# Reordering the first loads of a two-stage convolution kernel, and moving 18 outputs from its direct part to its triples

## The chip, the cores and the metric

One Trainium2 chip, one core. The metric is the device time of one execution in microseconds (us). Every profile shown is of one execution; its span is counted from the first instruction of the program to the last, and the execution's own time is a little longer than the span.

## The reference

Two 5-tap convolutions over time, each followed by GELU and by dropping every second output, then a joint network: projections of the result and of a second input `g`, their sum for every pair of positions, tanh, and an output projection.

```python
h = sum(einsum("btc,cd->btd", xp[:, i:i+T, :], w1[i]) for i in range(5))   # xp: x padded by 2
h = gelu(h)[:, ::2, :]
f = sum(einsum("btc,cd->btd", hp[:, i:i+T1, :], w2[i]) for i in range(5))  # hp: h padded by 2
f = gelu(f)[:, ::2, :]
fe, ge = f @ w_f, g @ w_g
out = tanh(fe[:, :, None, :] + ge[:, None, :, :]) @ w_o
```

Here B = 2, T = 4000, D = 512, 8 positions of `g`; the output is 2 x 1000 x 8 x 512 in bf16. T1 = 2000 and T2 = 1000.

## The kernel before

**Who does what.** TensorE (PE) does the matrix products, VectorE (DVE) and ScalarE (ACT) the sums, copies and nonlinear functions, GpSimd (POOL) memsets and sums late in the kernel, and the SyncE queue (SP) issues all loads and nearly all stores.

**An order made by a planner.** The program lists operations with what they read and write. `Plan` gives each a modelled cost, derives the dependencies, runs a list scheduler many times while it shifts priorities, and writes the resulting fixed order of instructions for each engine, with the semaphore waits that the dependencies need. Engines run their lists in order: an instruction that waits holds up everything behind it on its engine. So an edit in one place can change the order of ACT and DVE well after it.

**The first convolution in three kinds of parts.** Outputs of batch 0 begin with `ND` = 468 outputs computed directly, tap by tap (`direct`). The rest goes in triples: three outputs at a time by nine products in place of fifteen (`Triple` and `Unit`; the nine are t2, tm, sm, t1, s1, t0, s0, ti, si). A unit is one 128-wide slice of output channels of one triple part, four units to a part. The first, small triple part has `NF` = 176 columns a product (buffer `xa`), the second, `NL` = 336 columns (`xp1`), covers the end of batch 0. Batch 1 is two parts of 334 columns (`xp2`, then `xp0`). `NL` follows from the other two, `2 * 334 - ND / 3 - NF`.

**The direct part.** It needs samples with even and odd positions apart and channels on the partitions (`eo`). The samples come in two loads of 512 (`xr0`, `xr1`, called first and second samples here); each is transposed on PE (`turn(rt, pp, ...)`, `rt` the load, `pp` even or odd, eight transposes a call) and copied from PSUM to `eo`, in two halves of the channels, by DVE and ACT. Even taps need the even samples, odd taps the odd ones. `direct(i, lo, hi)` issues 16 matmuls (four output slices by four input slices) for tap `i` and outputs `lo` to `hi`. Outputs up to `NH` = 254 need the first samples alone.

**The order of the taps and loads.** `TAPS = (0, 4, 2, 1, 3)`. SP issues `xr0`, the weights of tap 0, `xr1`, the weights of tap 4, of tap 2, then transposing loads of `xa` with the weights of taps 1 and 3 among them, then those of `xp1`, `xp2` and `xp0` (six planes each), a small one called `xe` that holds the last samples of batch 1, and the weights of the second convolution. A load made with an `after` argument is issued only when an earlier load has landed: that of tap 4 waits for `xr0`, that of tap 2 for tap 0.

**Weights for the triples.** While PE is in the direct part, DVE and ACT combine the taps of `w1` into the weights that the triples use: `w1part(m, "04")` needs taps 0 and 4, `w1part(m, "213")` the others. They also form the sums of samples (`row` and the planes themselves, `Triple.step`).

**A unit's path.** t2 goes into a PSUM bank and ACT copies it out (`sd<-acc`); tm and sm are added to the bank and ACT copies it out again; t1 and s1 are added; DVE then forms the other two results (`acc<-acc,sd`, `sd<-acc,sd`), and t0, s0 and ti, si follow. Each step on PE needs the copy or sum before it. ACT's final function writes `hT`.

**The rest.** The second convolution (again triples, over `hT`), the projections and the joint network follow. Nothing of them is edited.

Of the kernel before, what the change touches and what calls it, by code (L numbers as in the profile page):

```python
# [360 lines left out]
def bass_standalone__seq2seq_rnn_t_joint__speech_kernel(  # L361
# [23 lines left out]
    assert (B, T, D, K, U) == (2, 4000, 512, 5, 8)  # L385
    T1, T2 = T // 2, T // 4
    NT3 = (T2 + 2) // 3
    ND, NF = 468, 176
    NL = 2 * NT3 - ND // 3 - NF
    assert ND % 6 == 0 and NF % 2 == 0 and NL % 2 == 0  # L390
    EW = 16 + 4 * P
# [7 lines left out]
    TAPS = (0, 4, 2, 1, 3)  # L399
    NX = 2  # L400

    with ExitStack() as es:
# [72 lines left out]
        pl = Plan(nc)  # L475
        sub, add = ALU.subtract, ALU.add

        def vec_cost(o, ins, fast=True):
            bf = fast and all(not v.psum and v.ap.dtype in (BF16, FP16) for v in (o,) + tuple(ins))
            return o.ap.free_size() * (0.52e-3 if bf else 1.04e-3) + 0.065  # L480
# [8 lines left out]
        def act(o, i, func, scale=1.0, bias=None):  # L489
            rd = (i,) if bias is None else (i, bias)  # L490
            pl.op("act", lambda e: e.activation(o.ap, i.ap, func, scale=scale,  # L491
                                                bias=0.0 if bias is None else bias.ap), rd, (o,),
                  o.ap.free_size() * 0.833e-3 + (0.05 if i.psum else 0.105 if bias is None else 0.186))

        def mm(o, pairs, start, stop, check=True):

            def fn(e):
                for n, (l, r) in enumerate(pairs):
                    ins = e.matmul(o.ap, lhsT=l.ap, rhs=r.ap, start=start and n == 0,  # L499
                                   stop=stop and n == len(pairs) - 1, skip_group_check=not check)  # L500
                return ins
            pl.op("pe", fn, [v for pr in pairs for v in pr], (o,), len(pairs) * max(o.ap.free_size() / 2400 + 0.0028, 0.056))
# [13 lines left out]
        def load_w(eng, dst, src, slack=0.0):  # L516
            return pl.dma(eng, lambda e: e.dma_start(dst.ap, src), (), (dst,), slack=slack)

        def load_xr(rt):
            dst = xr[rt][:].map(lambda a: a.rearrange("p r k c -> p (r k c)"))  # L520
            src = x[0, 4 * P * rt:4 * P * (rt + 1), :].rearrange("(p r) c -> p (r c)", r=4)
            return pl.dma("sp", lambda e: e.dma_start(dst.ap, src), (), (dst,), rate=370e3)

        def load_x6(buf, b, ph, j0, col, n=336, slack=1.0):

# [3 lines left out]
            return pl.dma("sp", lambda e: e.dma_start_transpose(out=dst.ap, in_=src), (), (dst,), nbytes=n * 2 * D, rate=175e3, slack=slack)  # L529

        came = [load_xr(0)]
        act(warm[0:1], warm[1:2], ACT.Gelu_apprx_tanh)

        def load_w1(i, after=None):
            o = load_w("sp", w1_sb[i], w1[i].rearrange("(k c) d -> c k d", c=P))
            if after is not None:
                o.after.append(after.idx)
            return o
# [3 lines left out]
        def load_a(*phs):  # L542
            for ph in phs:
                load_x6(xa, 0, ph, JA, 0, 16 * -(-(NF + 2) // 16), 0.8)

        came.append(load_w1(TAPS[0]))
        came.append(load_xr(1))
        for i in TAPS[1:3]:
            came.append(load_w1(i, came[-3]))
        load_a(4, 0)  # L550
        came.append(load_w1(TAPS[3], came[-3]))
        load_a(2)
# [33 lines left out]
        def turn(rt, pp, cost):  # L586
            for h in range(2):
                bk = 4 * (rt ^ pp) + 2 * h + 1
                pv = View(psb[:, bk * 1024:bk * 1024 + 512].rearrange("p (r k c) -> p r k c", r=2, k=2), np.array([bk]), True)

                def fn(e, pv=pv, h=h):
                    for k in range(2):
                        for r in range(2):
                            ins = e.transpose(pv.ap[:, r, k, :], xr[rt].h[:, 2 * r + pp, 2 * h + k, :], ident.h[:, :])  # L594
                    return ins
                pl.op("pe", fn, (xr[rt][:], ident[:]), (pv,), cost)
                lo = 16 + 2 * P * rt
                o = eo[pp, 2 * h:2 * h + 2, lo:lo + 2 * P].map(lambda a: a.rearrange("p k (c r) -> p k c r", r=2))
                v = pv.map(lambda a: a.rearrange("p r k c -> p k c r"))
                if h or rt and pp:  # L600
                    act(o, v, ACT.Copy)
                else:
                    pl.op("dve", lambda e, o=o, v=v: e.tensor_copy(out=o.ap, in_=v.ap), (v,), (o,), vec_cost(o, (v,)))
# [157 lines left out]
        NH = 2 * P - 2  # L761

        def direct(i, lo=0, hi=ND):
            for m in range(NK):
                mm(ps.cols(2 * m * NT + lo, hi - lo),
                   [(w1_sb[i, k, m * P:(m + 1) * P], eo[i % 2, k, 15 + i // 2 + lo:15 + i // 2 + hi]) for k in range(NK)],
                   i == TAPS[0] and lo == 0, i == TAPS[-1], False)
# [7 lines left out]
        turn(0, 0, 0.43)  # L775
        direct(TAPS[0], 0, NH)
        turn(0, 1, 0.43)
        turn(1, 0, 0.22)
        direct(TAPS[0], NH, ND)
        turn(1, 1, 0.22)  # L780
        for i in TAPS[1:]:
            direct(i)
        for m in range(NK):
            v = ps.cols(2 * m * NT, ND).map(lambda a: a.rearrange("p (q r) -> p r q", r=6))
# [503 lines left out]
```

## Time and profile before

| | |
|---|---|
| runs | 253.19, 253.51, 252.77 us |
| median | 253.19 us |
| profiled execution | 253.5 us, its span 251.7 us |
| granted TensorE clock | 0.999 |
| PE busy | 246.3 us, 98% of the span |
| DVE, ACT busy | 211.8 and 211.7 us, 84% each |
| POOL busy | 97.5 us, 39% |
| moved by DMA | 31.99 MB, mean 127 GB/s; 234, 277 and 241 GB/s in the first three of 40 slices, 6.3 us each |

How to read the views: "PE" is TensorE's matmuls, "PEld" its weight loads, which run beside them. A row of the timeline gives start, length, engine, line, operation, output and inputs with partitions and elements, and in brackets how long the engine had been idle and what ended that. The chain of waits goes back from the last instruction, at each step to what released it. All helper matmuls have line 499, all ACT functions line 491. A row's length is from start to end; instructions of one engine overlap at their ends, so what a step costs its engine is the distance between starts.

### The profile page before, as it was taken

To read this page: it belongs to the slowest core of one execution; us is meant where nothing else is said; L and a number is where in the kernel's file an instruction comes from. 1 tells how busy PE (TensorE), PEld (TensorE's weight loads), DVE (VectorE), ACT (ScalarE), POOL (GpSimd) and SP (SyncE) were. 2 spreads that over 40 slices of the span, in tenths; PEclk is the share of its full clock that TensorE was granted. 3 is DMA by queue.
4 is the path that set the end of the run, shared out by engine and by line. 5 is a ranking of instruction groups with operands and counts; after the bars stand their busy time and mean duration, and the time that the engine had idled before them with its cause. 6 is when DMAs were issued, how large, how long until landed. Compare 5 with 4: busy or idle time off the path is not lost.

```text
span 251.7 us, 5281 instructions
## 1 busy us (share of the span) xinstructions
PE 246.3 (98%) x1909; PEld 180.3 (72%) x1915; DVE 211.8 (84%) x354; ACT 211.7 (84%) x356; POOL 97.5 (39%) x105
## 2 busy tenths in 40 slices
PE   8999999999999999999999999999999999999995
PEld 4646986666666666667556878777888878787883
DVE  2699998965999999398966878899999995889773
ACT  3496999659968766984499999999999999999872
POOL 1000000000000000000006987879999998878750
PEclk9999999999999999999999999999999999999999
DMA  6999999998300034000001033432335365555457
GB/s 234 277 241 189 175 146 154 182 171 297 125 0 3 0 112 142 0 1 3 0 0 39 5 128 108 133 99 83 126 118 177 128 212 193 180 183 177 147 172 226
DMA packets 55159, 31.99 MB, mean 127 GB/s; under 512 B 32062, under 2 KB 54878, under 8 KB 55134
## 3 DMA queue, kind: packets, MB, share of 16 engines
q1 hardware_dynamic: 54846, 31.47, 47.6%
q8 instruction: 15, 0.25, 0.4%
q10 hardware_dynamic: 288, 0.20, 0.3%
q14 instruction: 10, 0.08, 0.1%
HBM read 7.86 MB, written 16.38 MB: 96 GB/s over the span
## 4 chain that ended last, share of the span: by engine, by line
PE 73%; ACT 16%; issue 4%; DMA 4%; SPq 1%; DVE 1%; POOL 0%; ACTq 0%; DVEq 0%
PE acc L499 73%; ACT sn L1016 4%; DMA xr<-in_x_dram 3%; ACT jX L491 2%; ACT jT L491 2%; ACT row L491 2%; ACT sd L491 1%; ACT og L1016 1%; DMA xe<-in_x_dram 1%; SPq L529 1%; ACT ost L1016 1%; ACT hT L491 1%; DVE og L486 1%; ACT xp L491 0%; PE acc L594 0%
## 5 line engine op out<-in xcount | busy, mean ns | idle before, releaser
L486 DVE TENSOR_TENSOR og<-acc,sn 128x512 bf16<-128x512 f32 x84 | 55.0, 684 | 10.6 <-PE acc L499 8.9
L491 ACT ACTIVATE jT<-feT,geT 128x1000 bf16<-128x1000 f32 (+6 forms) x56 | 52.7, 1003 | 0.3 <-DVE feT L486 0.3
L499 PE MATMUL acc<-tw,ss 128*128 128x256 f16 x336 | 46.1, 273 | 0.1
L1079 POOL TENSOR_TENSOR ss<-jT 128x512 f16<-128x512 bf16 x25 | 29.0, 1169 | 38.9 <-DVE ss L1079 37.6
L499 PE MATMUL acc<-row,w_sb 128*128 128x334 bf16 (+2 forms) x224 | 38.8, 295 | 0.0
L499 PEld LDWEIGHTS acc<-tw,ss 128*128 128x128 f16 x336 | 32.4, 98 | 7.5 <-ACT sn L1016 0.5
L1016 ACT ACTIVATE sn<-acc 128x512 f32<-128x512 f32 x51 | 33.1, 655 | 2.6 <-PE acc L499 1.7
L499 PE MATMUL acc<-wo_sb,jT 128*128 128x256 bf16 (+1 forms) x187 | 31.3, 292 | 0.3
L499 PEld LDWEIGHTS acc<-row,w_sb 128*128 128x128 bf16 x224 | 21.1, 97 | 9.5 <-DVE acc L606 0.9
L491 ACT ACTIVATE jX<-feT,geT 128x1000 bf16<-128x1000 f32 (+4 forms) x28 | 25.2, 970 | 0.0
L1017 DVE COPY sn<-acc 128x512 f32<-128x512 f32 x33 | 22.2, 684 | 2.7 <-PE acc L499 2.4
L483 POOL MEMSET hT<- 128x8 bf16 (+2 forms) x6 | 0.8, 149 | 59.1 <-ACT hT L491 43.1
L499 PEld LDWEIGHTS acc<-wo_sb,jT 128*128 128x128 bf16 x192 | 18.7, 98 | 6.1
L491 ACT ACTIVATE hT<-acc 128x334 bf16<-128x334 f32 (+3 forms) x36 | 15.2, 438 | 9.0 <-PE acc L499 8.8
L491 ACT ACTIVATE sd<-acc 128x334 f32<-128x334 f32 (+2 forms) x48 | 19.7, 431 | 3.5 <-PE acc L499 2.8
L606 DVE SCALAR_TENSOR_TENSOR acc<-acc,sd 128x334 f32<-128x334 f32 (+2 forms) x24 | 11.6, 483 | 10.1 <-PE acc L499 10.0
L1079 POOL TENSOR_TENSOR ss<-jX 128x512 f16<-128x512 bf16 x16 | 18.5, 1159 | 3.5 <-DVE ss L1079 3.5
L486 DVE TENSOR_TENSOR row<-row 128x1336 bf16<-128x1336 bf16 (+2 forms) x24 | 19.0, 795 | 0.0
L499 PE MATMUL acc<-xp,w_t 128*128 128x334 bf16 (+1 forms) x96 | 17.6, 305 | 0.0
L499 PE MATMUL acc<-hT,w_t 128*128 128x334 bf16 x96 | 17.6, 304 | 0.0
L499 PE MATMUL acc<-wo_sb,ss 128*128 128x256 bf16 x112 | 17.0, 273 | 0.0
L499 PE MATMUL acc<-xp,w_x 128*128 128x334 bf16 (+1 forms) x96 | 16.9, 305 | 0.0
(124 smaller groups left out, 512.3 us busy)
## 6 DMA issues: line engine op xcount, KB each, us to landing
out_dram<-og SPq DMA_DIRECT2D x98, 128.0 KB, 2.0
w_sb<-in_w_dram SPq DMA_DIRECT2D x10, 512.0 KB, 5.7
out_dram<-ost SPq DMA_DIRECT2D x10, 128.0 KB, 1.9
xr<-in_x_dram SPq DMA_DIRECT2D x2, 512.0 KB, 4.8
wf_sb<-in_w_f_dram SPq DMA_DIRECT2D x1, 512.0 KB, 3.6
wg_sb<-in_w_g_dram SPq DMA_DIRECT2D x1, 512.0 KB, 4.7
wo_sb<-in_w_o_dram SPq DMA_DIRECT2D x1, 512.0 KB, 5.8
xp<-in_x_dram SPq DMA_TRANSPOSE x18, 4.8
```

Of the source, the lines that this page charges most:

```text
L483: pl.op("pool", lambda e: e.memset(v.ap, 0.0), (), (v,))
L486: pl.op(eng, lambda e: e.tensor_tensor(out=o.ap, in0=a.ap, in1=b.ap, op=op), (a, b), (o,), 0.02 + 2.14e-3 * o.ap.free_size() if eng == "po ...
L491: pl.op("act", lambda e: e.activation(o.ap, i.ap, func, scale=scale, bias=0.0 if bias is None else bias.ap), rd, (o,), o.ap.free_size() * ...
L499: ins = e.matmul(o.ap, lhsT=l.ap, rhs=r.ap, start=start and n == 0, stop=stop and n == len(pairs) - 1, skip_group_check=not check)
L529: return pl.dma("sp", lambda e: e.dma_start_transpose(out=dst.ap, in_=src), (), (dst,), nbytes=n * 2 * D, rate=175e3, slack=slack)
L606: pl.op(eng, lambda e: e.scalar_tensor_tensor(out=o.ap, in0=a.ap, scalar=f, in1=b.ap, op0=ALU.mult, op1=add), (a, b), (o,), vec_cost(o, (a ...
L1016: pl.flex({"act": (lambda e: e.activation(o.ap, v.ap, ACT.Copy), 0.05 + n * 0.833e-3), "dve": (lambda e: e.tensor_copy(out=o.ap, in_=v.ap) ...
L1017: "dve": (lambda e: e.tensor_copy(out=o.ap, in_=v.ap), 0.065 + n * 1.04e-3)}, (v,), (o,))
L1079: fn = lambda e, o=S[i], x=x, y=y, op=op: e.tensor_tensor(out=o.ap, in0=x.ap, in1=y.ap, op=op)
```

## The change

Three edits that go together. The load of tap 4's weights moves ahead of the load of the second samples, and it no longer waits for a load; the load of the second samples now waits until the first samples have landed. Tap 4's products are split at output 254 as tap 0's are, and its first half is listed ahead of the transposes of the second samples. And 18 outputs go from the direct part to the small triple part: 468 to 450 direct outputs, 176 to 182 columns; `NL` stays 336.

```diff
-    ND, NF = 468, 176
+    ND, NF = 450, 182
...
-        def load_xr(rt):
+        def load_xr(rt, after=None):
...
-            return pl.dma("sp", lambda e: e.dma_start(dst.ap, src), (), (dst,), rate=370e3)
+            o = pl.dma("sp", lambda e: e.dma_start(dst.ap, src), (), (dst,), rate=370e3)
+            if after is not None:
+                o.after.append(after.idx)
+            return o
...
         came.append(load_w1(TAPS[0]))
-        came.append(load_xr(1))
-        for i in TAPS[1:3]:
-            came.append(load_w1(i, came[-3]))
+        came.append(load_w1(TAPS[1]))
+        came.append(load_xr(1, came[-3]))
+        came.append(load_w1(TAPS[2], came[-3]))
...
         turn(0, 0, 0.43)
         direct(TAPS[0], 0, NH)
         turn(0, 1, 0.43)
+        direct(TAPS[1], 0, NH)
         turn(1, 0, 0.22)
+        turn(1, 1, 0.22)
         direct(TAPS[0], NH, ND)
-        turn(1, 1, 0.22)
-        for i in TAPS[1:]:
+        direct(TAPS[1], NH, ND)
+        for i in TAPS[2:]:
             direct(i)
```

In the order that the planner makes of it, PE runs the 16 transposes of the first samples, 32 matmuls of 254 outputs, the 16 transposes of the second samples, 32 matmuls of 196, 48 of 450, and then the triples. DVE makes four of the weight sums of taps 0 and 4 before its copy of the second samples. SP has the same list but for the two loads; POOL has the same list. On PE the order of the products of the first two triple parts differs in places and is the same from about the eighth unit on; on ACT and DVE single instructions stand a few places earlier or later until the end of the first convolution. After that all lists are the same.

## The prediction

> **What bounds the kernel now.** The page comes first: PE is busy nearly all the time, so what can be won is PE work, or the few places where PE waits.
>
> ```profile
> PE 246.3 (98%) x1909; PEld 180.3 (72%) x1915; DVE 211.8 (84%) x354; ACT 211.7 (84%) x356; POOL 97.5 (39%) x105
> ```
>
> Then the chain of waits in order of time, for the first 27 us: the end hangs on the load of the second samples (landed at 7.97), their transposes, an ACT copy, and then PE.
>
> ```profile
> 1.65 6.32 DMA xr<-in_x_dram
> ...
> 8.10 0.62 PE acc L594 x8
> ...
> 8.75 0.61 ACT eo L491
> ...
> 9.40 14.65 PE acc L499 x84
> ```
>
> Then PE's timeline, for the prices. 64 matmuls of 176 columns start from 27.05 to 31.93, 0.0763 us apart; 8 of 336 start from 31.93 to 33.08, 0.144 apart; so a column costs 0.00042 us.
>
> ```profile
> 5.89 1.93 PE L499 MATMUL acc<-eo,w_sb 128*128 128x254 bf16 x16
> 23.57 1.08 PE L499 MATMUL acc<-xa,w_x 128*128 128x176 bf16 x12
> 26.74 0.48 PE L499 MATMUL acc<-row,w_t 128*128 128x176 bf16 x4 [0.16 <-ACT sd L491]
> 27.05 0.47 PE L499 MATMUL acc<-xa,w_t 128*128 128x176 bf16 x4
> 31.93 1.31 PE L499 MATMUL acc<-xp,w_x 128*128 128x336 bf16 x8
> 33.08 0.47 PE L499 MATMUL acc<-row,w_sb 128*128 128x176 bf16 x4
> ```
>
> Last the chain from 54 to 67.5 us and ACT's timeline there. The last small load of the first convolution (`xe`) lands at 57.50, POOL copies it, ACT can start its two-plane `row` only then, and ACT works without a pause until PE, at 67.53, gets the copy it waited for.
>
> ```profile
> 54.38 3.12 DMA xe<-in_x_dram
> ...
> 57.55 0.28 POOL xp L572
> ...
> 67.53 2.58 PE acc L499 x17
> ```
> ```profile
> 57.85 2.44 ACT L491 ACTIVATE row<-xp 128x2688 bf16<-128x2688 bf16 x1
> 60.20 0.77 ACT L491 ACTIVATE hT<-acc 128x336 bf16<-128x336 f32 x2
> 60.86 0.45 ACT L491 ACTIVATE sd<-acc 128x334 f32<-128x334 f32 x1
> 61.19 0.53 ACT L491 ACTIVATE hT<-sd 128x334 bf16<-128x334 f32 x1
> 61.59 2.46 ACT L491 ACTIVATE row<-hT 128x2688 bf16<-128x2688 bf16 x1
> 63.92 0.47 ACT L491 ACTIVATE sd<-acc 128x334 f32<-128x334 f32 x1
> 64.25 0.48 ACT L491 ACTIVATE hT<-acc 128x334 bf16<-128x334 f32 x1
> 64.58 1.36 ACT L491 ACTIVATE xp<-xp 128x1336 bf16<-128x1336 bf16 x1
> 65.79 1.35 ACT L491 ACTIVATE row<-row 128x1336 bf16<-128x1336 bf16 x1
> 67.00 0.48 ACT L491 ACTIVATE sd<-acc 128x334 f32<-128x334 f32 x1
> ```
>
> **PE work.** From the spacing, 254 columns cost 0.109 us, 214 0.0923, 196 0.0847; 468 costs 0.1985, since 16 of 214 and 64 of 468 fill 9.40 to 23.57; so 450 costs 0.191. Direct part before: 16 x 0.109 + 16 x 0.0923 + 64 x 0.1985 = 15.92. After: 32 x 0.109 + 32 x 0.0847 + 48 x 0.191 = 15.37, 0.55 less, though it has 16 matmuls more. The small triple part has 144 matmuls with 6 columns more: +0.36. Net -0.19.
>
> A weight load's row lasts 0.097 us, longer than the 0.0763 between matmuls of 176, so loads are covered at 196 columns too. The Trainium skill ("TensorE: Matmul & The Clock Gate", section "Back-to-back issue gap") speaks against this: it has a stream of weight loads and matmuls sustain about 81 ns a matmul at 128 columns and 131 ns at 512. By straight lines between these the direct part would grow from 11.05 to 11.89 us and the triples by 0.11, in all +0.95; the rows above, closer at 176 and wider at 468, do not follow it.
>
> **The waits at the start.** PE finishes tap 0's first half at 5.89 + 1.74 = 7.63 and starts the second samples' transposes at 8.10; these take 0.89, and the next matmul starts at 9.40. So 0.47 and 0.41 are idle. After the change tap 4's half (1.74) stands in the first gap. Its weights take the place in the queue in which the second samples landed at 7.97. Loads one and two landed at 4.06 and 5.56, 1.50 apart, so a third without stragglers lands at 7.06: bounds 7.06 and 7.97. I take 7.4 and no wait; at the late end the wait of 0.47 stays. Tap 4's half ends at 9.37 to 9.84.
>
> The second samples are now issued when the first have landed (4.08), where tap 4's load was, which landed at 9.34 (5.3 us after issue). The bounds are 7.06 + 1.50 = 8.56 and, with the third load's 2.41 once more, 7.97 + 2.41 = 10.4. I take 9.34. Transposes to next matmul is 1.30 (8.10 to 9.40), so the second halves start at 10.7 to 11.8. DVE now has four weight sums ahead of its copy of the second samples: they wait for tap 4 and start every 0.605 us (9.36, 9.97, 10.57, 11.18), so the copy starts 2.5 us after tap 4 lands and ends at 10.6 to 11.2; behind it are PE's second halves. I take 11.0. With 2.71 + 9.17 to go the direct part ends at 22.9, not 23.57: 0.67 earlier; bounds 1.0 earlier and 0.1 later. The later taps are no limit: tap 2 landed at 11.06 and is needed at 13.7, taps 1 and 3 at 15.68 and 17.88, needed at 16.8 and 19.8. SP passes nothing else: its list from the weights of tap 2 on is the old one.
>
> **The triples, 23 to 57 us.** +0.36. PE's wait of 0.34 at 26.74 (ACT runs a 1.2 us `row` ahead of the copy) I put at 0.2, since one GELU now stands ahead of it. Of the wait of 0.2 at 42.22 little should be left, as the order now has another unit's products there. Against that DVE, back to back from 9.36 to about 35, is only its one early sum (0.6) ahead, so PE, coming 0.67 earlier, meets it at about two places; I put these at 0.3, bounds 0 and 0.6. Gain by 55 us: 0.67 - 0.36 + 0.14 + 0.2 - 0.3 = 0.35; bounds 0.9 and -0.7.
>
> **The cap at 57 to 67 us.** When `xe` lands does not depend on PE: SP issues the plane loads without a pause from 17.97 to 55.6. So ACT's two-plane `row` starts at 57.85 as before. One `hT` that stood behind it now stands ahead of it, where ACT has the room if PE is 0.17 early. The steps from there to the copy at 67.00 become 2.35 + 0.33 + 0.33 + 0.40 + 2.33 + 0.33 + 0.33 + 1.21 + 1.21 = 8.82: the copy starts at 66.67, and PE goes on at 67.20 in place of 67.53. More than 0.33 does not pass; less than that comes only if PE's gain falls under 0.08, as PE idled 0.25 there. After it PE has no gap over 0.05 until 126 us and the lists hold the same work, so 0.33 is carried to the end.
>
> **Sum.** 253.5 - 0.33 = 253.17 for the profiled execution, which is 0.31 above the median of the three runs; for the median 252.85. A measurement of this kernel can tell about 0.3%, 0.76 us, from no change.
>
> **Rivals.**
> (1) The cap gives way. If `xe` lands 0.3 to 0.7 us earlier, PE's own gain passes with the 0.25: -0.6 to -1.1, about 252.3. For it: the transposing loads' issues vary between 1.3 and 4.2 us, so a queue that begins otherwise can end otherwise. Against it: SP's list and bytes are the same. 0.30.
> (2) Nothing comes of it: tap 4 lands at 7.97, the wait of 0.47 only changes its name, and the 0.36 of the triples and DVE's delays eat the rest: 0 to -0.2, about 253.1. 0.13.
> (3) The other side: the second samples come late. Their place is now fourth, and all 16 transposes, 32 half products and 48 whole ones wait behind them. The direct part ends 13.3 us after they land, so from a landing at 10.3 it ends later than before; the fifth load landed at 11.06, and with that it ends at 24.4, 0.8 late. With +0.36, less the waits that it would fill (0.34, 0.25), this gives 0.55 to 0.9: 253.7 to 254.1. Against it: this place landed at 9.34. 0.14.
> (4) Weight loads are not covered in the halves: 16 x 0.098 = 1.57 more, less 0.67, with 0.36 and less the filled waits of 0.79 makes +0.5: 253.7. The 0.0763 spacing speaks against it; 0.03. The Trainium skill's spacing would give 254.1.
> That the change does not do what it says is out: the lists of instructions have it.
>
> **Numbers.** Forecast 0.40, rivals 0.30, 0.13, 0.14, 0.03. Faster by over 0.3% is under 252.43: most of (1) and a little of the forecast, 0.30. Slower by over 0.3% is over 253.95: part of (3) and (4), and runs whose `xe` is late by as much as (1) has it early, 0.16. The rest 0.54. The forecast's own range is 252.6 to 253.1; with (1), (2) and the nearer half of (3) it is 252.1 to 253.8.
>
> **What would show it.** Tap 4's first half starts at 7.6 to 8.1 with no idle over 0.5 ahead; transposes at 9.4 to 9.9; the first matmul of 182 columns near 22.9; 182 columns spaced 0.079; `xe` landing near 57.5; PE going on after an ACT copy near 67.2 and the span 251.4. Wrong would be: the second samples after 10.3, matmuls of 196 spaced over 0.09, new idle of PE over 0.5 between 26 and 57, or a 67.2 that moves with something other than `xe`.

## The result, and the profile after

The changed kernel takes 252.98 us (median of 22 runs, 252.29 to 253.58); the kernel before, on the same chip, takes 253.39 (22 runs). The ratio is 0.9982, 95% interval 0.9975 to 0.9988: 0.41 us faster, inside the band of 0.3% that the prediction could not tell from no change, though the interval leaves no change out. Two later comparisons gave 252.78 (0.9978, 0.9968 to 0.9988) and 252.80 (0.9975, 0.9966 to 0.9983). The forecast was 252.85. The profiled execution took 252.52 us, its span 250.7; the one of before took 253.5, span 251.7.

First the page's line of busy times, after:

```profile
PE 245.7 (98%) x1931; PEld 181.4 (72%) x1931; DVE 212.0 (85%) x354; ACT 212.0 (85%) x356; POOL 97.4 (39%) x105
```

The shares barely move. The chain of waits of the first 72 us after does:

```profile
1.19 4.54 DMA w_sb<-in_w_dram
...
5.97 3.66 PE acc L499 x32
9.63 0.46 PE acc L597 x8
...
10.11 0.61 ACT eo L491
...
10.76 61.29 PE acc L499 x486
```

Two first halves run as one block from 5.97, the second samples' transposes follow without a gap, one wait of 0.41 us for ACT's copy is left ahead of 10.76, and then PE alone carries the chain to the end of the window. ACT's `row` and the load of `xe`, which stood on the chain of before, are gone from it.

PE's timeline after gives the places that the prediction named:

```profile
22.66 1.11 PE L499 MATMUL acc<-xa,w_x 128*128 128x182 bf16 x12
25.62 0.49 PE L499 MATMUL acc<-row,w_t 128*128 128x182 bf16 x4
25.94 0.48 PE L499 MATMUL acc<-xa,w_t 128*128 128x182 bf16 x4
41.36 0.73 PE L499 MATMUL acc<-row,w_sb 128*128 128x336 bf16 x4
66.50 0.74 PE L499 MATMUL acc<-row,w_t 128*128 128x334 bf16 x4
```

The first triple matmul starts at 22.66 (23.57 before). The `row,w_t` at 25.62 and the `row,w_sb` at 41.36, which waited 0.33 and 0.20 us before, wait 0.04 and nothing. The `row,w_t` that started at 67.53 starts at 66.50: 1.03 us earlier. From there to the last ACT instruction the two profiles lie a constant 1.0 us apart; nothing later gives it back.

And around `xe` (POOL's and ACT's timelines after):

```profile
54.49 0.26 POOL L575 COPY xp<-xe 128x16 bf16<-128x16 bf16 x1 [15.59 <-DMA xe<-in_x_dram]
```
```profile
55.26 1.32 ACT L491 ACTIVATE row<-xp 128x1344 bf16<-128x1344 bf16 x1
56.49 0.43 ACT L491 ACTIVATE sd<-acc 128x334 f32<-128x334 f32 x1
56.82 0.44 ACT L491 ACTIVATE hT<-acc 128x336 bf16<-128x336 f32 x1
57.15 2.44 ACT L491 ACTIVATE row<-xp 128x2688 bf16<-128x2688 bf16 x1
```

`xe` landed at 54.44, not 57.50. ACT reached its two-plane `row` at 57.15 through its own list, 2.4 us after POOL had the samples. The cap that the prediction put there did not hold.

### The profile page after: what moved, and what is told of

It is laid out like the page before. It is cut to its first block, busy times and chain, and to the rows that moved or that the text cites. A ratio compares the mean times of both kernels' runs of the same rounds, so it can differ in the third digit from the quotient of the medians.

```text
span 250.7 us, 5316 instructions
## 1 busy us (share of the span) xinstructions
PE 245.7 (98%) x1931; PEld 181.4 (72%) x1931; DVE 212.0 (85%) x354; ACT 212.0 (85%) x356; POOL 97.4 (39%) x105
## 4 chain that ended last, share of the span: by engine, by line
PE 83%; ACT 10%; issue 3%; DMA 2%; DVE 1%; SPq 0%; ACTq 0%; DVEq 0%
PE acc L499 83%; ACT sn L1021 4%; ACT jX L491 2%; DMA w_sb<-in_w_dram 2%; ACT og L1021 1%; ACT jT L491 1%; ACT ost L1021 1%; DVE og L486 1%; ACT eo L491 0%; PE acc L597 0%; SPq L522 0%; ACT ost L491 0%; DVE ss L1084 0%; ACTq L322 0%; DVEq L322 0%
## 5 line engine op out<-in xcount | busy, mean ns | idle before, releaser
L499 PE MATMUL acc<-wo_sb,jT 128*128 128x256 bf16 (+1 forms) x192 | 32.1, 295 | 0.0
```

## The experiments

Theory A is the prediction's: `xe` lands late whatever PE does, and cuts the gain at 57 to 67 us. Theory B: `xe` is early enough, and the gain is PE's own. Theories C, D and E, on where the gain of the parts goes, came with the second and third group. The kernel before ran beside each group: 253.37, 253.45 and 253.31 us.

**1. Does `xe` hold the kernel?** The changed kernel again, then two kernels that issue `xe` ahead of the six plane loads of `xp0`, and one that issues it later. Only SP's list is edited; the lists of the other engines stay:

```diff
+        sp = order["sp"]
+        sp.remove(self.small)                      # xe
+        sp.insert(sp.index(self.first), self.small)       # early; late: + 6 + 2
...
```

The changed kernel again:

> The changed kernel once more, for a second profile beside the others of this call. Theory A (the prediction): the gain of the first 24 us, 0.9 in the profile of after, is cut at 57 to 67 us by the landing of xe and ACT's list behind it; in the profile of after xe landed at 54.4 and cut nothing, so other executions must have it later, between 55 and 58. Theory B: xe never holds the changed kernel, and the time is lost elsewhere. Ratio to before 0.998 in both. If this profile has xe after 57, A expects PE to go on near 67.2; B expects 66.5 whatever xe does.

Measured 252.78, ratio 0.9978 (0.9968 to 0.9988). `xe` landed at 54.39, PE's landmark (the `row,w_t` of 67.53 before) came at 66.64.

The kernel before with `xe` early:

> The kernel before, with the small load xe issued ahead of the six plane loads of xp0 instead of behind them; all other engines' lists unchanged. A: PE's wait of 0.25 at 67.5 shrinks or goes, ACT's two-plane row no longer starts after POOL's copy but after ACT's own list: 0.1 to 0.4 us faster than before, ratio 0.9985 to 0.9995. B: no change, ratio 0.9997 to 1.0003.

Measured 253.25, ratio 0.9997 (0.9989 to 1.0006). `xe` landed at 43.95; the landmark moved from 67.53 to 67.25. PE's wait for ACT's copy there shrank from 0.24 to 0.08, which is 0.16 of these 0.28 us; the triples also started 0.19 earlier in this execution (23.38 against 23.57; the second samples landed at 7.78 against 7.97), and other small differences take 0.07 back. So the late `xe` cost the one profiled execution of before about 0.16 us, and the median nothing that these runs show.

The changed kernel with `xe` early:

> The changed kernel, with xe issued ahead of the six plane loads of xp0; all other engines' lists unchanged. A: what is cut in the executions with a late xe passes: 0.2 to 0.5 us faster than the changed kernel, 252.5 to 252.8, ratio to before 0.996 to 0.9975. B: the same as the changed kernel, ratio 0.998.

Measured 252.90, ratio 0.9985 (0.9976 to 0.9994), landmark at 66.65: no better than the changed kernel. `xe` does not hold it, and theory A falls for this kernel.

The changed kernel with `xe` behind two weight loads of the second convolution:

> The changed kernel, with xe issued behind two weight loads of the second convolution (1.5 us each) instead of ahead of them; all other engines' lists unchanged. xe lands about 3 us later, 57.4 to 60.5. A: ACT's two-plane row starts 0.35 us after the landing and every us over 57.2 is passed on to PE: 0.5 to 3 us slower than the changed kernel, ratio to before 1.000 to 1.010. B, if ACT has more room than the prediction gave it: under 0.3 slower.

Measured 253.90, ratio 1.0020 (1.0006 to 1.0035). Its chain of waits between 50 and 70 us (helpers have other line numbers here):

```profile
51.46 6.40 DMA xe<-in_x_dram
...
57.91 0.27 POOL xp L579
...
58.21 0.48 ACT row L494
...
67.54 2.58 PE acc L502 x17
```

With `xe` landing at 57.86 the chain of before is back, and the landmark at 67.54. The mechanism of the cap is real; its condition is not met. In the ten executions that were profiled with `xe` in its old place, apart from the one of before, it landed at 54.1 to 56.3. Two of the ten have the old load order (54.06 and 54.78, from the kernels with the new sizes alone below), so the earlier landing is no gain of the new order: the 57.50 was the exception.

**2. One part at a time.** The load order and split with the old sizes, the new sizes with the old order, the changed kernel a third time, and the sizes moved on. The planner makes a list of its own for each:

```diff
-    ND, NF = 450, 182        # changed kernel
+    ND, NF = 468, 176        # order alone
+    ND, NF = 426, 190        # sizes moved on
-    ND, NF = 468, 176        # kernel before
+    ND, NF = 450, 182        # sizes alone
```

> The changed kernel with the old sizes (468 direct outputs, triples of 176): only the load order and the split of both taps' products. Theory B (the gain is PE's own: less waiting at the start, and fewer columns; nothing later gives it back): the direct part has 16 matmuls of 254 in place of 16 of 468 split in two, so its work is 15.97 against 15.92 us, and the wait of 0.47 us ahead of the second samples' transposes is gone. The first triple matmul comes near 23.1 us (23.57 before), and 0.3 to 0.5 us of that are left at the end: 252.9 to 253.1, ratio 0.9980 to 0.9992. Theory A (what is won at the start is cut at 57 to 67 us by the load of xe): at most 0.33 is left, ratio 0.9987 to 1.000. Theory C (order and sizes only help together, because the triples of 176 come too early for ACT's first row): ratio 0.9995 to 1.0005, with PE's wait near 26.5 us at 0.5 us or more in place of 0.33.

Measured 253.56, ratio 1.0009 (0.9999 to 1.0019). The profiled execution, 253.14, is the fastest of the twelve, so its rows do not show what the median lost.

> The kernel before with the new sizes only (450 direct outputs, triples of 182), loads and tap order as before. Theory B: the direct part loses 64 x 18 columns at 0.00042 us = 0.48 us and the triples gain 0.36, the waits of 0.47 and 0.41 us at the start stay, and the longer triples may fill part of the wait of 0.33 at 26.7 us: 0.1 to 0.4 us faster, 253.0 to 253.3, ratio 0.9984 to 0.9996. Together with the run of the order alone it should add up to the whole change's 0.4 to 0.6 us. Theory A: as much, up to its 0.33. Theory C: 0.9995 to 1.0005.

Measured 253.62, ratio 1.0010 (1.0001 to 1.0018): a little slower than before, if at all.

> The changed kernel once more, as the reference for the two parts on the same chip, and a third sample of where xe lands. Both theories: 252.8 to 253.0, ratio 0.9975 to 0.9985. Theory B: xe lands anywhere from 54 to 57.5 us, and PE at the unit after it follows PE's own work unless xe lands after 57. Theory A: xe lands near 57.5 and PE waits for ACT's copy behind it.

Measured 252.80, ratio 0.9975 (0.9966 to 0.9983); `xe` landed at 56.00 and the landmark came at 66.41.

> The changed kernel, with the sizes moved on: 426 direct outputs and triples of 190. By the columns alone: 32 second halves of 172 in place of 196 (32 x 24 x 0.00042 = 0.32 less), 48 of 426 in place of 450 (0.48 less), 144 triple matmuls of 190 in place of 182 (144 x 8 x 0.00042 = 0.48 more): 0.32 us less, 252.5 to 252.7, ratio 0.9965 to 0.9980 if PE's columns decide. If the copies and sums of ACT and DVE for the longer triples come late, the gain goes into new waits between 23 and 57 us: 252.8 to 253.2, ratio 0.9978 to 0.9995.

Measured 252.60, ratio 0.9972 (0.9963 to 0.9981): as fast as the changed kernel beside it, the intervals overlap.

Neither part gains anything alone; together they gain 0.65 us here. That the parts add up, as theory B had it, falls; theory C is nearest to what was seen. What eats into the parts stands in PE's rows. The order alone meets ACT, as C had it, though the wait was 0.40 and not over 0.5:

```profile
25.78 0.48 PE L499 MATMUL acc<-row,w_t 128*128 128x176 bf16 x4 [0.23 <-ACT sd L491]
```

(The bracket counts from the modelled end of the matmul ahead; by starts the wait is 0.40.) The sizes alone meet DVE twice, here PE's two rows and DVE's three:

```profile
31.27 0.49 PE L499 MATMUL acc<-row,w_sb 128*128 128x182 bf16 x4 [0.38 <-DVE acc L606]
35.87 1.31 PE L499 MATMUL acc<-row,w_x 128*128 128x336 bf16 x8 [0.19 <-DVE row L486]
```
```profile
29.31 1.63 DVE L486 TENSOR_TENSOR row<-row,xp 128x1352 bf16<-128x1352 bf16 x2
30.86 0.34 DVE L606 SCALAR_TENSOR_TENSOR acc<-acc,sd 128x182 f32<-128x182 f32 x1
...
34.97 0.84 DVE L486 TENSOR_TENSOR row<-row 128x1344 bf16<-128x1344 bf16 x1
```

The `acc` that PE needs at 30.7 stands behind two sums of planes. The waits by starts are 0.55 and 0.36.

**3. Lists or sizes?** An operation has the same number in kernels that differ in sizes alone, so one kernel can run the list of another. The planner's search is left out and its result for the other sizes written in:

```diff
-        order = self.schedule(pred)
+        order = {e: list(v) for e, v in LISTS.items()}   # the other kernel's lists
+        self.start = STARTS                              # and its planned starts
...
```

> The load order and the tap split with the old sizes (468, 176) again, but every engine runs the changed kernel's list of operations, written out, in place of the list that the planner makes for these sizes. Theory D (the loss of the order alone lies in its list: the waits of 0.40, 0.20, 0.16, 0.13 and 0.10 us between 23 and 42 us come from which product and which sum stands next): by columns it has 0.24 us more PE work than the changed kernel (direct part +0.60, triples -0.36) and otherwise its waits of about 0.5: 252.9 to 253.2, ratio 0.9980 to 0.9993. Theory E (the old sizes themselves cost it: triples of 176 run ahead of ACT and DVE whatever the list): 253.4 to 253.7, ratio 1.000 to 1.0015, with some 1 us of waits between 23 and 42 us.

Measured 253.13, ratio 0.9990 (0.9981 to 0.9999).

> The changed kernel (450, 182) with the lists that the planner makes for 468 and 176 under the new load order. Theory D: the lists carry the waits; 0.8 to 1.1 us of waits between 23 and 42 us in place of 0.5, 253.0 to 253.4, ratio 0.9985 to 0.9999. Theory E: the lists do not matter, it runs as the changed kernel: 252.7 to 252.9, ratio 0.9970 to 0.9982.

Measured 253.88, ratio 1.0017 (1.0008 to 1.0026).

> The old load order with the new sizes (450, 182) and the lists of the kernel before. Theory D: the waits of 0.55 and 0.36 us that the sizes alone had at 31 and 35.5 us are not there, since no two sums of planes stand ahead of the sum that PE waits for; waits between 23 and 42 us about the 0.7 of the kernel before, the columns 0.2 less: 253.0 to 253.3, ratio 0.9983 to 0.9996. Theory E: 253.5 to 253.7, ratio 1.0003 to 1.0018.

Measured 253.46, ratio 1.0006 (0.9997 to 1.0015).

> The sizes moved on (426, 190) with the changed kernel's lists. If one list serves sizes this near, the columns decide: 0.32 us under the changed kernel, 252.4 to 252.6, ratio 0.9962 to 0.9972, as with its own lists. If a list has to be made for its sizes: new waits of 0.3 to 0.7 us between 23 and 42 us, 252.8 to 253.2, ratio 0.9975 to 0.9990.

Measured 253.23, ratio 0.9990 (0.9981 to 0.9999).

The first two decide for theory D against E. On one chip, the old sizes with the changed kernel's lists are 0.75 us faster than the new sizes with the lists made for the old ones, though by columns they have 0.24 us more work. The 253.88 lies above D's own range too (253.0 to 253.4): the waits came to 1.37, where D had at most 1.1, and with tap 4 landing at 8.15 the triples started at 23.31 in place of 22.66. What a list does is seen in PE's and DVE's rows of the second of these kernels:

```profile
25.96 0.49 PE L513 MATMUL acc<-row,w_t 128*128 128x182 bf16 x4 [0.21 <-ACT sd L505]
28.06 0.49 PE L513 MATMUL acc<-row,w_sb 128*128 128x182 bf16 x4 [0.35 <-DVE acc L623]
```
```profile
26.71 0.70 DVE L500 TENSOR_TENSOR ssum<-wv,w_sb 128x512 f32<-128x512 f32 x1
27.31 0.43 DVE L500 TENSOR_TENSOR w_t<-w_sb 128x512 bf16<-128x512 bf16 x1
27.64 0.36 DVE L623 SCALAR_TENSOR_TENSOR acc<-acc,sd 128x182 f32<-128x182 f32 x1
```

and in DVE's rows of the changed kernel:

```profile
26.25 0.68 DVE L486 TENSOR_TENSOR ssum<-wv,w_sb 128x512 f32<-128x512 f32 x1
26.86 0.34 DVE L609 SCALAR_TENSOR_TENSOR acc<-acc,sd 128x182 f32<-128x182 f32 x1
27.11 0.41 DVE L486 TENSOR_TENSOR w_t<-w_sb 128x512 bf16<-128x512 bf16 x1
```

One weight sum has changed places with the `acc` that PE waits for, which makes up 0.33 us of the 0.52 that PE waits, by starts, ahead of 28.06. PE's list differs too: the changed kernel has two more groups (`row,w_x` and `xa,w_x`, eight matmuls, 0.63 us) ahead of the `row,w_t` at 25.62, which give ACT time for its copy; the other list has not, and waits 0.37 at 25.96.

The last two were misses for a plain "one good list serves all". Before's lists at the new sizes (253.46, outside D's range and next to E's) lose as much as the planner's own, in another place (PE's and DVE's rows):

```profile
26.05 0.49 PE L513 MATMUL acc<-xa,w_x 128*128 128x182 bf16 x4 [0.56 <-DVE w_x L500]
```
```profile
25.57 0.41 DVE L500 TENSOR_TENSOR w_x<-w_sb 128x512 bf16<-128x512 bf16 x1
```

With the old load order DVE makes this `w_x` at 25.57, as before (25.61), but PE now comes 0.8 us earlier and waits 0.73 by starts. The changed kernel's lists at 426 and 190 wait for the same `w_x`, 0.70 us; there tap 4 landed at 8.07, and DVE made it at 25.28 in place of 24.71, so how much is the list and how much the landing is open.

All of it adds up in one table. "Start" is the first triple matmul, "waits" all gaps of PE between it and the landmark that are over 0.04 us longer than the usual spacing of that shape, "landmark" the `row,w_t` at 67.53 before; all in us, from one profile each. "Rest" is landmark less start less waits.

| kernel | start | waits | landmark | rest |
|---|---|---|---|---|
| before | 23.57 | 0.98 | 67.53 | 42.98 |
| before, `xe` early | 23.38 | 0.85 | 67.25 | 43.02 |
| order alone | 23.12 | 1.12 | 67.22 | 42.98 |
| order alone, changed kernel's lists | 23.76 | 0.35 | 67.11 | 43.00 |
| sizes alone | 22.81 | 1.29 | 67.45 | 43.35 |
| sizes alone, lists of before | 22.79 | 1.28 | 67.39 | 43.32 |
| changed | 22.66 | 0.50 | 66.50 | 43.34 |
| changed, again | 22.96 | 0.37 | 66.64 | 43.31 |
| changed, third | 22.58 | 0.50 | 66.41 | 43.33 |
| changed, lists of the order alone | 23.31 | 1.37 | 68.01 | 43.33 |
| changed, `xe` early | 22.76 | 0.56 | 66.65 | 43.33 |
| changed, `xe` late | 22.82 | 1.39 | 67.54 | 43.33 |
| 426 and 190 | 22.25 | 0.60 | 66.67 | 43.82 |
| 426 and 190, changed kernel's lists | 22.42 | 0.87 | 67.16 | 43.87 |

The rest depends on the columns alone: 43.0 at 176, 43.3 at 182, 43.8 at 190. What differs between kernels of one size is the start and the waits, and only the whole change (at 182 or at 190 columns, with lists of its own) has both an early start and few waits. Under the new load order the waits go with the lists at either size: at 176 columns 1.12 with the planner's own and 0.35 with the changed kernel's, at 182 columns 0.37 to 0.56 with the changed kernel's (but for the late `xe`) and 1.37 with those of the order alone. The exchanged lists ran where tap 4 landed later (8.02 and 8.15, against 7.11 to 7.81), so their starts are not compared at like landings. From the landmark to the end every one of these executions takes 185.9 to 186.4 us.

## Why the prediction was right, and where it was not

**PE work: right.** Spacing came out at 0.109 (254 columns), 0.084 (196), 0.190 (450) and 0.079 us (182), against 0.109, 0.0847, 0.191 and 0.0788 forecast; the triples' 0.36 is the difference of 43.34 and 42.98 in the table. Rival (4) did not happen. The sustained figures of the Trainium skill ("TensorE: Matmul & The Clock Gate", section "Back-to-back issue gap") do not agree with these rows: an estimate by straight lines between its 81 ns at 128 columns and 131 ns at 512 gives 0.090 us at 196 columns and 0.123 at 450.

**The start: right in its order, better than the taken values.** Tap 4 landed at 7.35 (7.4 taken), the second samples at 8.65 (9.34 taken), inside the bounds; DVE's copy ended at 10.58, ahead of ACT's at 10.72, so the second halves started at 10.76 and the direct part ended 0.91 earlier, not 0.67. In the two other executions of this kernel it ended at 22.96 and 22.58. Later landings of tap 4 exist: 7.81 in one of these two and up to 8.15, beyond the prediction's bound of 7.97, in other kernels with the new load order. From 7.81 on they leave 0.2 to 0.6 us of wait ahead of tap 4's half. In the six executions with a landing at 7.67 or later DVE's copy did come last, as the prediction had it: with the landing at 7.81 it ended at 10.93, ACT's at 10.85, and the second halves started at 11.08.

**The triples: the step that was mis-sized.** The prediction gave DVE a lead of one sum, 0.6 us, and charged 0.3 us for PE meeting it. DVE's first weight sum and the `w_x` that PE can meet at 25 us show the lead, before and then after:

```profile
9.36 0.69 DVE L606 SCALAR_TENSOR_TENSOR wu<-w_sb 128x512 f32<-128x512 bf16 x1
25.61 0.42 DVE L486 TENSOR_TENSOR w_x<-w_sb 128x512 bf16<-128x512 bf16 x1
```
```profile
7.37 0.69 DVE L609 SCALAR_TENSOR_TENSOR wu<-w_sb 128x512 f32<-128x512 bf16 x1 [1.21 <-DMA w_sb<-in_w_dram]
24.71 0.41 DVE L486 TENSOR_TENSOR w_x<-w_sb 128x512 bf16<-128x512 bf16 x1
```

DVE starts 2.0 us earlier. By 10.72 it has four sums and the copy done; before it had two sums and the copy done at 10.57, and its fifth sum came at 11.78. The lead is 0.9 us at `w_x`, the same as PE's 0.91, so PE's waits for DVE stay small, 0.13 us at most (at 31.86): all waits up to the landmark fell from 0.98 to 0.50; between 23 and 57 us from 0.74 to 0.42, where the prediction took 0.34 away and added 0.3. By 57 us the gain is therefore 0.91 - 0.36 + 0.32 = 0.87, where 0.35 was forecast by 55. Sizes alone, with the lists of before, show what PE meets without that lead: 0.73 at the same `w_x`. Order alone moves both engines, but its lists put PE's needs in the wrong places.

**The cap at 57 to 67 us: wrong.** The step took the landing of `xe` at 57.5 from one execution as fixed. Its own rival (1) named the way out, issues of transposing loads of 1.3 to 4.2 us; the profile shows that rival, -1.03 at the landmark where at most 0.33 was to pass. The runs with `xe` early and late show both halves: no gain from an earlier `xe`, +1.1 us (253.90 against 252.78) when it lands at 57.9.

**The time: close by luck.** What happened in the profile is rival (1), given 0.30; the time that came out is the forecast's. Both mis-sized steps made the gain too small: the three profiles of the changed kernel lie at 252.52, 252.75 and 252.57, 0.75 to 0.98 below that of before, where 0.33 was forecast. The medians gain only 0.41 to 0.65. A part of the difference is that the profile of before was an execution with a late `xe` and a later start than the one with `xe` early: beside that one's 67.25, the landmark's gain is 0.61 to 0.84. The other part, some 0.2 us, is not settled; all three profiles of the changed kernel lie below their medians (252.98, 252.78, 252.80), by 0.03 to 0.46, so one profile each is too little for it. And the forecast of 252.85 started from 253.19, the median of three runs, where 22 runs have 253.39: 0.20 too low, against a gain that was 0.07 too small, leaves the 0.13 by which it missed 252.98. Rivals (2) and (3) are out for the changed kernel: its three starts were 0.61 to 0.99 earlier, and the second samples landed before 9.6 in every execution with the new load order. The condition of (2) is met elsewhere: with tap 4 at 8.15 and the lists of the order alone, the new sizes started only 0.26 earlier than before, at 23.31. That the two edits go together, which the prediction summed term by term, was not seen: its terms for load order and for sizes, taken alone, would each have promised a gain, and each alone gave none.

## What to carry to other kernels

Where a planner writes the order, an edit of a size or of a load is also an edit of every list after it. Test the parts with the lists held fixed as well as with lists of their own, or a part's worth and a new order's luck are taken for one another. Where two engines are back to back behind the same data (PE and DVE here), moving one earlier gains only as far as the other moves with it; look which load starts the second one. A landing time seen in one execution is a sample: before it is used as a bound, ask how long each issue ahead of it can take.

## What was not expected of the hardware

The same SP list brought `xe` in at 54.4 to 56.0 us in three executions of the changed kernel. The issues of the same transposing loads took 1.3 to 4.2 us each on SP; one execution had two of 3.4 us (at 28.2 and 40.8) and landed at 56.0, where 57.50 belongs to the execution of before with one of 4.2 and one of 3.1. What makes an issue long was not tried. The third load of the queue landed anywhere from 7.1 to 8.15 us, at 7.11 to 7.91 in the three kernels of the second group that have the new load order, and at 8.02 to 8.15 in the three of the third group, which ran on another chip; whether the chip makes that was not tried.
